# Attention, soft experts and a gated layer on one core: the gated layer's scale chain rewritten and its order of work redrawn

## The chip, the cores and the metric

One core of one Trainium2 chip runs the whole program. The metric is the time of one execution on the device in microseconds (us).

## What is computed

Three layers follow each other. Inputs of the first two are float32, the weights of the third are float64.

```python
# attention, 4 batches x 12 heads x 448 x 64, causal
scores = where(mask, -1e9, q @ k.T / 8);  attn = softmax(scores) @ v
x = attn as 1792 tokens x 768
# soft mixture: 8 experts x 4 slots
logits = x @ phi
slot_out[e] = relu((softmax(logits, 0).T @ x)[e] @ w1[e]) @ w2[e]     # 32 slots x 768
x = c @ slot_out,  c = softmax(logits, 1)                             # 1792 x 32
# gated layer, 1536 hidden columns
gate = sigmoid(x @ w_gate);  val = x @ w_val
out = (gate * val) @ w_out
```

## The kernel before, in words

The first 230 us are attention, the next 70 us the experts, whose weights stream in from memory, and the rest is the gated layer, which the change is about. The work of attention and of the gated layer is not written in the order in which it runs. A class `Plan` (L20) holds a list of operations, each with its engines and a cost in us, its dependencies, the buffers that it takes and a due time. `play` (L41) hands them out one by one and pins that order on each engine. For the gated layer a table `GSHIFT` (L163) shifts the due times, and with them the order; three numbers `SLACK, MARGIN, WAIT` set how due times go backwards and how far a later operation may be preferred. Costs and table decide the order and nothing else: on the chip each engine runs its list and waits where an operand or a buffer is late.

**The gated layer** runs over 6 units u of 256 hidden columns. Since x is c @ slot_out, the gate's and the value's weights are first multiplied with slot_out, once per unit:

- *Conversion.* Each unit has three weight blocks, o (w_out), v (w_val) and g (w_gate), of 1.5 MB float64. They land in a ring of five buffers (`ld`, by SP). ScalarE (`a1`, `a2`) and VectorE (`d1`, `d2`) turn each into float32 in place, four passes over 128x1536 words, which the trace shows as `w<-w`. A block's load waits until the block that had its buffer is used up: the load of unit 5's g block waits for `wlo` of unit 4.
- *Scale chain*, per unit: `psg` on TensorE (both products as four partial sums), `mv` on VectorE (largest absolute value of each row, for g and for v), `am2` (those two maxima as bf16), `one2` on TensorE (a matrix of ones times the maxima, so that each partition has the sum of all), `pw2` on VectorE (`pow2`, L251: the power of two below that sum, p, and the scale s = 2^14/p), then `ag` and `osc`, two small products of p for later. Beside it `gh` on ScalarE copies `psg` to SBUF and `fld` on TensorE folds the four partial sums. `sth` (ScalarE) and `stl` (VectorE) make of that sum a float16 pair, the tile `st`.
- For w_out: `absw` on ScalarE, `am` (its maximum as bf16), `one`, `pw`, then the float16 pair `whi` (ScalarE) and `wlo` (VectorE).
- *Hidden blocks.* Each unit has four batches b of 448 tokens with two blocks c of 128 hidden columns. `gv` on TensorE gives gate and value (`psg`, `psv` in the trace, 448 columns each), `sig` (ScalarE) the sigmoid, `hsv` (VectorE) the product `hs`, `hhi` (ScalarE) its upper half in float16 and `hlo` (GpSimd) the lower one. `hs` has two buffers, so a block's `hsv` waits for the `hlo` two blocks ahead of it.
- *Out-tiles.* 14 tiles i of 128 tokens: `outp` is 12 matmuls of 384 columns (`pso`), three products hhi·wh, hhi·wl and hlo·wh for both blocks. In unit 0 the first six come in two parts, with the hlo products last. Each half of the result is emptied by `evict`: in units 1 to 4 one half goes by ScalarE into a tile `ev` (two buffers), which `addp` on GpSimd adds to `oacc`, and the other half is added by VectorE. In the last unit both go by VectorE and each tile is stored.

Behind `psg` of unit 0, TensorE runs 20 products of ones (`psf`), which fill the wait for the first scale chain.

Of the kernel before, what the change touches and what calls it, by code (L numbers as in the profile page):

```python
# [101 lines left out]
def kernel(  # L102
# [60 lines left out]
    GSHIFT = {('a1', 1): 23.4, ('a1', 2): -6.21, ('a1', 3): 117.66, ('a1', 4): -5.02, ('a1', 5): 53.58, ('a2', 1):  # L163
              20.66, ('a2', 2): 118.34, ('a2', 3): 123.22, ('a2', 4): 79.78, ('a2', 5): 4.11, ('absw',): 36.12,
              ('addp', 1): 9.2, ('addp', 2): -5.3, ('addp', 3): -47.55, ('addp', 4): 58.74, ('am',): 1.36, ('am2',):
              -23.99, ('d1', 1): -180.16, ('d1', 2): 54.75, ('d1', 3): -2.65, ('d1', 4): -1.62, ('d1', 5): 30.01,
              ('d2', 1): 9.59, ('d2', 2): -33.11, ('d2', 3): -32.37, ('d2', 4): 8.67, ('d2', 5): 0.27, ('evict', 0):
              -148.33, ('evict', 1): -68.2, ('evict', 2): -111.03, ('evict', 3): -19.74, ('evict', 4): -31.48,
              ('evict', 5): 19.57, ('fl',): -9.57, ('fld',): 25.66, ('gh',): -29.78, ('gv', 0): -10.56, ('gv', 1):
              -235.77, ('gv', 2): -71.57, ('gv', 3): 21.32, ('gv', 4): 9.31, ('gv', 5): 8.04, ('hhi', 0): -461.87,  # L170
              ('hhi', 1): 83.0, ('hhi', 2): 5.44, ('hhi', 3): 25.33, ('hhi', 4): -7.65, ('hhi', 5): 9.17, ('hlo', 0):
              -0.95, ('hlo', 3): -9.74, ('hlo', 4): 42.9, ('hlo', 5): 20.64, ('hsv', 0): 17.3, ('hsv', 1): -5.98,
              ('hsv', 2): 0.18, ('hsv', 3): -20.78, ('hsv', 4): 18.54, ('hsv', 5): 4.2, ('ld', 1): -6.69, ('ld', 2):
              23.28, ('ld', 3): -32.29, ('ld', 4): -2.0, ('ld', 5): 39.32, ('mv',): -42.04, ('one',): -118.12,
              ('one2',): -17.53, ('outp', 0): 65.58, ('outp', 1): 1.02, ('outp', 10): 136.03, ('outp', 11): -0.62,
              ('outp', 12): -6.35, ('outp', 2): -3.63, ('outp', 3): 123.94, ('outp', 4): -8.45, ('outp', 5): -18.09,
              ('outp', 6): 218.04, ('outp', 7): -1.03, ('outp', 8): 231.97, ('outp', 9): 108.01, ('psg',): -384.17,
              ('pw',): -22.44, ('pw2',): -103.76, ('sig', 0): -240.48, ('sig', 1): -4.63, ('sig', 2): 27.87, ('sig',
              3): -144.49, ('sig', 4): -20.28, ('sig', 5): 17.06, ('sth', 0): -26.98, ('sth', 1): -11.12, ('sth', 2):
              -2.93, ('sth', 3): -40.58, ('sth', 4): -4.7, ('sth', 5): -0.58, ('stl', 0): 3.56, ('stl', 1): -0.2,  # L180
              ('stl', 2): 25.38, ('stl', 3): 8.1, ('stl', 4): -61.65, ('stl', 5): 13.43, ('store', 0): -10.25,
              ('store', 1): 15.69, ('store', 10): 2.55, ('store', 11): 55.39, ('store', 12): 11.05, ('store', 13):
              2.24, ('store', 2): 10.3, ('store', 3): 3.04, ('store', 4): -40.57, ('store', 5): 29.87, ('store', 6):
              7.57, ('store', 7): 43.43, ('store', 8): -4.75, ('store', 9): 49.48, ('whi',): -12.54, ('wlo',): 19.95}
# [1000 lines left out]
    def prep(u):  # L1185
        for nm in "ovg" if u else "":
# [22 lines left out]
        op((mv, u), call(mv), {"V": 0.8}, [(psg, u)], use=[p1])  # L1209
# [1 line left out]
        op((fld, u), call(fld), {"P": 0.9}, [(gh, u)], new=[("a", p2)], use=[h])
        op((am2, u), call(am2), {"V": 0.15}, [(mv, u)])
        op((one2, u), call(one2), {"P": 0.04}, [(am2, u)], new=[("b", x)])
# [90 lines left out]
```

## Time and profile before

| | |
|---|---|
| median of 3 runs | 519.91 us (519.75 to 521.16) |
| profiled execution, its own time | 519.79 us |
| its span in the profile | 518.0 us |
| TensorE busy, matmuls | 470.9 us (91%) |
| VectorE, ScalarE, GpSimd busy | 378.0, 341.4, 277.9 us |
| gated layer | about 300 to 518 us |

The span runs from the first to the last recorded instruction; the execution's own time has 1.8 us more around it. Nearly every gated instruction goes through one wrapper, line 244, so the rows are told apart by their tiles: `pso` is an out-tile, `w<-w` a conversion pass, `oacc` or `ev` an eviction, `mgv` is `mv`, `am` a cast of maxima, `gv4p` and `gv4s` the p and s of unit 4's pair, `o4p` and `o4s` those of its w_out. A row of the list in order of time gives start, duration, engine, operation, tiles out<-in, count, and in brackets the idle time before it with what ended it.

### The profile page before, as it was taken

What the parts mean: (1) busy time and instruction counts of PE and PEld (TensorE: products, weight loads), DVE (VectorE), ACT (ScalarE), POOL (GpSimd) and SP (SyncE); (2) the same over time, 40 slices, a digit from 0 to 9 for tenths busy, and PEclk for the clock granted to TensorE, in tenths of its full rate; (3) what the DMA queues carried; (4) which work ended last, traced back from release to release, by engine and by line L of the source; (5) the groups of instructions that cost most, each with busy time, mean ns of one, the idle gap of its engine ahead of it and who ended that gap; (6) DMA issues with size and microseconds to landing.
All of it is one profiled execution on the core that took longest, in us unless ns stands there. A gap on an engine that the chain in (4) does not pass through costs nothing.

```text
span 518.0 us, 12116 instructions
## 1 busy us (share of the span) xinstructions
PE 470.9 (91%) x4516; PEld 293.0 (57%) x4516; DVE 378.0 (73%) x920; ACT 341.4 (66%) x759; POOL 277.9 (54%) x371
## 2 busy tenths in 40 slices
PE   3899999999999999999837578999999998999997
PEld 2667767767667776655412234555455554555554
DVE  3889888989988987621055049899798998978564
ACT  3788887989887886111081059999897897686330
POOL 3088777787768812000000007249699997997530
PEclk9999999999999999999985999999999999999999
DMA  6866776762767357899999993360553320300145
GB/s 149 200 167 190 202 218 156 176 186 62 220 154 191 123 154 279 331 416 424 410 409 424 412 395 139 114 253 0 163 204 121 139 106 1 124 0 1 53 178 196
DMA packets 87531, 101.55 MB, mean 196 GB/s; under 512 B 68656, under 2 KB 68912, under 8 KB 85424
## 3 DMA queue, kind: packets, MB, share of 16 engines
q1 hardware_dynamic: 86544, 100.55, 57.4%
q8 instruction: 35, 0.57, 0.5%
q10 hardware_dynamic: 928, 0.23, 0.2%
q14 instruction: 24, 0.20, 0.1%
HBM read 95.26 MB, written 5.51 MB: 195 GB/s over the span
## 4 chain that ended last, share of the span: by engine, by line
PE 54%; POOL 15%; DMA 12%; DVE 6%; ACT 6%; issue 6%; SPq 1%; POOLq 0%; ACTq 0%; DVEq 0%
PE pso L244 11%; PE psP L244 8%; PE psS L244 8%; PE psV L244 7%; DMA w<-in_moe_w_gate_dram 5%; POOL hlo L244 5%; POOL oacc L244 5%; DMA w<-in_moe_w_dram 5%; POOL sq L244 4%; PE so L1069 3%; PE psT L244 3%; PE psh L1056 3%; PE psY L244 2%; PE psX L244 2%; ACT w L244 2%
## 5 line engine op out<-in xcount | busy, mean ns | idle before, releaser
L244 POOL TENSOR_TENSOR hlo<-hs,hhi 128x448 f16<-128x448 f32 x47 | 69.8, 1494 | 124.7 <-ACT hhi L244 124.6
L244 PEld LDWEIGHTS <-hhi 128*128 128x128 f16 x672 | 65.2, 98 | 51.1 <-issue 7.9
L244 ACT ACTIVATE P<-psS,nm 128x384 f32<-128x384 f32 (+3 forms) x168 | 82.1, 505 | 11.4 <-DVE nm L244 8.7
L244 PE MATMUL pso<-wh,hhi 128*128 128x384 f16 x336 | 82.7, 326 | 1.0 <-ACT oacc L244 0.5
L244 POOL TENSOR_TENSOR oacc<-oacc,ev 128x384 f32<-128x384 f32 x56 | 76.4, 1381 | 11.7 <-ACT ev L244 10.3
L244 PE MATMUL pso<-wh,hlo 128*128 128x384 f16 x336 | 81.6, 326 | 0.9 <-POOL hlo L244 0.9
L244 PE MATMUL pso<-wl,hhi 128*128 128x384 f16 x336 | 82.4, 326 | 0.0
L244 DVE CUSTOM_DVE_ANT_0 psS<-psS,cmaskq,sc 128x128 f32<-128x128 f32 (+2 forms) x144 | 62.8, 487 | 3.1 <-PE psS L244 2.4
L244 DVE SCALAR_TENSOR_TENSOR oacc<-pso,osc,oacc 128x384 f32<-128x384 f32 x84 | 50.1, 611 | 18.5 <-PE pso L244 18.2
L244 DVE SCALAR_TENSOR_TENSOR w<-w 128x1536 int32<-128x1536 int32 x30 | 62.0, 2067 | 0.7 <-ACT w L244 0.7
L244 PE MATMUL psP<-ident,P 128*128 128x128 f32 x384 | 59.4, 282 | 1.3 <-ACT P L244 1.3
L244 POOL TENSOR_TENSOR sq<-sq 112x512 bf16<-112x512 bf16 (+1 forms) x80 | 51.1, 639 | 6.0
L244 PEld LDWEIGHTS psP<-ident,P 128*128 128x128 f32 x384 | 42.9, 142 | 15.2 <-issue 8.8
L244 ACT COPY PT<-psP 128x512 f32<-128x512 f32 x83 | 46.7, 587 | 6.3 <-PE psV L244 5.2
L244 PE MATMUL psS<-qT,qT 64*64 64x256 f16 (+3 forms) x1008 | 48.9, 294 | 1.5 <-ACT qT L244 0.7
L244 ACT ACTIVATE w<-w 128x1536 int32<-128x1536 uint16 (+1 forms) x30 | 49.3, 1647 | 1.3 <-DMA w<-in_moe_w_gate_dram 1.3
L244 PE MATMUL psV<-PT,v 128*64 128x448 f32 (+3 forms) x384 | 46.8, 386 | 0.0
L244 ACT ACTIVATE ev<-pso,osc 128x384 f32<-128x384 f32 x56 | 32.7, 584 | 21.1 <-PE pso L244 11.1
L244 PEld LDWEIGHTS <-hlo 128*128 128x128 f16 x336 | 32.7, 98 | 23.2 <-POOL hlo L244 1.3
L327 DVE TENSOR_SCALAR hm<-psh,emask 128x256 f32<-128x256 f32 x8 | 5.3, 662 | 46.7 <-PE psh L1056 44.2
L244 PEld LDWEIGHTS <-qT 64*64 64x64 f16 x1008 | 28.2, 108 | 19.5 <-issue 7.0
L1064 ACT COPY hT<-psht 128x256 f32<-128x256 f32 x8 | 3.0, 372 | 53.6 <-PE psht L1062 46.8
(252 smaller groups left out, 847.7 us busy)
## 6 DMA issues: line engine op xcount, KB each, us to landing
w<-in_moe_w_dram SPq DMA_DIRECT2D x32, 1536.0 KB, 9.5
w<-in_moe_w_out_dram SPq DMA_DIRECT2D x6, 1536.0 KB, 11.8
w<-in_moe_w_val_dram SPq DMA_DIRECT2D x6, 1536.0 KB, 13.6
w<-in_moe_w_gate_dram SPq DMA_DIRECT2D x6, 1536.0 KB, 6.6
q<-in_q_dram SPq DMA_DIRECT2D x48, 112.0 KB, 3.3
k<-in_k_dram SPq DMA_DIRECT2D x46, 112.0 KB, 3.4
out_dram<-oacc SPq DMA_DIRECT2D x13, 384.0 KB, 2.3
v<-in_v_dram SPq DMA_DIRECT2D x36, 128.0 KB, 3.2
```

Of the source, the lines that this page charges most:

```text
L244: x = f(*a, **kw)
L327: nc.vector.tensor_scalar(to.rearrange("s (i q) -> s q i", i=2), ps.rearrange("s (q i) -> s q i", i=2), 0.0, emask[:, e:e + 1], ALU.max, A ...
L1056: nc.tensor.matmul(ps[32 * g:32 * g + 32, :], lhsT=slotT[:, kc, :], rhs=w[:, kc % 3, 256 * g:256 * g + 256], start=kc == 0, stop=kc == KC - 1)
L1064: nc.scalar.copy(hT, pt)
L1069: nc.tensor.matmul(so[32 * c:32 * c + 32, :], lhsT=hT[:, i, 32 * g:32 * g + 32], rhs=w[:, f % 4, 256 * c:256 * c + 256], start=e == 0 and ...
```

## The change

Six things are changed, all of them in the gated layer.

1. `pow2` works in PSUM: maximum, bit mask and reciprocal are written next to the ones' product, in the bank in which it landed, and only s goes to SBUF. The copy of p to SBUF is a fifth instruction, which for the pair g, v is put off into a new step `pw3`, with `ag` and `osc`.
2. `mv` writes its maxima as bf16, and `am2` is gone.
3. `am` (w_out's maximum as bf16) goes from VectorE to ScalarE.
4. `one2` is issued ahead of `fld`, always.
5. `sig` is planned behind `pw3`, since `ag` now comes from there.
6. The plan's costs, its three numbers and the table of shifts are new, so the whole order of the gated layer is drawn anew. The program up to `psg` of unit 0 keeps its order, but for unit 0's own w_out scale.

```diff
-    SLACK, MARGIN, WAIT = 1.252, 0.894, 0.49
-    GSHIFT = {('a1', 1): 23.4, ('a1', 2): -6.21, ('a1', 3): 117.66, ('a1', 4): -5.02, ('a1', 5): 53.58, ('a2', 1):
...
+    SLACK, MARGIN, WAIT = 0.213, 0.838, 0.347
+    GSHIFT = {('a1', 1): 46.98, ('a1', 2): 72.49, ('a1', 3): 117.45, ('a1', 4): 76.85, ('a1', 5): 11.54, ('a2', 1):
...
     def pow2(pool, mx, n, nm):
-
+        m, r = mx[:, :n], mx[:, n:]
         p = pool.tile([128, n], F32, tag=nm + "p", name=nm + "p")
         s = pool.tile([128, n], F32, tag=nm + "s", name=nm + "s")
-        on.ve.tensor_scalar(p, mx, 2.0 ** -20, None, ALU.max)
-        on.ve.tensor_scalar(p.bitcast(I32), p.bitcast(I32), 0x7F800000, None, ALU.bitwise_and)
-        on.ve.reciprocal(s, p)
-        on.ve.tensor_scalar(s, s, P14, None, ALU.mult)
-        return p, s
+        on.ve.tensor_scalar(m, m, 2.0 ** -20, None, ALU.max)
+        on.ve.tensor_scalar(m.bitcast(I32), m.bitcast(I32), 0x7F800000, None, ALU.bitwise_and)
+        on.ve.reciprocal(r, m)
+        on.ve.tensor_scalar(s, r, P14, None, ALU.mult)
+        return p, s, lambda: on.ve.tensor_copy(p, m)
...
     def am(nm, u):
         x = unit[u]["am", nm] = sm2.tile([128, 1], BF16, tag="am" + nm, name="am")
-        on.ve.tensor_copy(x, unit[u]["m", nm])
+        on.ac.copy(x, unit[u]["m", nm])
...
     def mv(u):
         d = unit[u]
-        d["mgv"] = sm2.tile([128, 2], F32, tag="mgv", name="mgv")
+        d["mgv"] = sm2.tile([128, 2], BF16, tag="mgv", name="mgv")
         on.ve.tensor_reduce(d["mgv"], d["ps"], axis=AX.X, op=ALU.max, apply_absolute_value=True)
-    def am2(u):
-        x = unit[u]["am2"] = sm2.tile([128, 2], BF16, tag="am2", name="am2")
-        on.ve.tensor_copy(x, unit[u]["mgv"])
-
     def one2(u):
-        x = unit[u]["x2"] = ps1.tile([128, 2], F32, tag="b", name="amx2")
-        on.te.matmul(x, lhsT=ones, rhs=unit[u]["am2"], start=True, stop=True)
+        x = unit[u]["x2"] = ps1.tile([128, 4], F32, tag="b", name="amx2")
+        on.te.matmul(x[:, :2], lhsT=ones, rhs=unit[u]["mgv"], start=True, stop=True)
     def pw2(u):
         d = unit[u]
-        p, r = pow2(sm2, d.pop("x2"), 2, f"gv{u}")
+        d["pgv"], r, d["f"] = pow2(sm2, d.pop("x2"), 2, f"gv{u}")
         for c, nm in enumerate("gv"):
-            d["p", nm], d["s", nm] = p[:, c:c + 1], r[:, c:c + 1]
+            d["s", nm] = r[:, c:c + 1]
+    def pw3(u):
+        d = unit[u]
+        d.pop("f")()
+        p = d["pgv"]
+        for c, nm in enumerate("gv"):
+            d["p", nm] = p[:, c:c + 1]
         d["ag"] = sm1(f"ag{u}")
         on.ve.tensor_scalar(d["ag"], p[:, 0:1], 2.0 ** -28, None, ALU.mult)
         osc(u)
...
-                op((am, u), lambda e: am("o", u), {"V": 0.15}, [(absw, u)])
+                op((am, u), lambda e: am("o", u), {"A": 0.2}, [(absw, u)])
...
+        op((one2, u), call(one2), {"P": 0.04}, [(mv, u)], new=[("b", x)])
+        op((fld, u), call(fld), {"P": 0.9}, [(gh, u)], new=[("a", p2)], use=[h], behind=[(one2, u)])
         op((pw2, u), call(pw2), {"V": 0.8}, [(one2, u)], use=[x])
+        op((pw3, u), call(pw3), {"V": 0.42}, [(pw2, u)], use=[x])
```

Three places show how rows move. The first is TensorE's list behind `psg` of unit 0, where `amx` is the ones' product `one2`, the `psg` made of `gh` is `fld`, and `psf` are the filling products.

```order
-L244 MATMUL psg_4744<-gh,fold_66 128x512
-L244 LDWEIGHTS ones
-L244 MATMUL amx_4751<-am_4749,ones 128x2
 L244 LDWEIGHTS ones
 L244 MATMUL psf<-ones 128x256
...
+L244 MATMUL amx_4751<-mgv,ones 128x2
+L244 MATMUL psg_4753<-gh,fold_66 128x512
```

The ones' product now takes `mgv` itself and stands ahead of the fold instead of behind it. Seven filling products stand ahead of the two and thirteen behind.

The second place is VectorE's list from the first hidden blocks of unit 0: `hs` is a hidden block, `w` a conversion pass, `hlo` a lower half. Before:

```order
L244 SCALAR_TENSOR_TENSOR hs<-psv,sg 128x448 x2
L244 SCALAR_TENSOR_TENSOR w<-w 128x1536
L244 TENSOR_TENSOR hlo<-hs,hhi 128x448
L244 SCALAR_TENSOR_TENSOR hs<-psv,sg 128x448 x2
L244 TENSOR_SCALAR oacc<-pso,osc_4763 128x384 x2
```

Now:

```order
L244 SCALAR_TENSOR_TENSOR hs<-psv,sg 128x448 x2
L244 SCALAR_TENSOR_TENSOR w<-w 128x1536
L244 SCALAR_TENSOR_TENSOR hs<-psv,sg 128x448
L244 SCALAR_TENSOR_TENSOR w<-w 128x1536
L244 SCALAR_TENSOR_TENSOR hs<-psv,sg 128x448
```

Batch 0's second `hlo` has left VectorE and runs on GpSimd behind the first one; a second conversion pass has come up into its place. On TensorE, `gv` of batch 2's first block now stands between the two parts of the first out-tile.

The third place is VectorE's list around the scale chain of unit 4, where the two `hs` are batch 3's blocks of unit 3. Before:

```order
L244 SCALAR_TENSOR_TENSOR hs<-psv,sg 128x448
L244 CAST am<-mo 128x1
L244 SCALAR_TENSOR_TENSOR oacc<-pso,osc_5920,oacc 128x384
L244 SCALAR_TENSOR_TENSOR hs<-psv,sg 128x448
L244 TENSOR_REDUCE mgv<-psg 128x2
L244 CAST am_6197<-mgv 128x2
L244 TENSOR_SCALAR o4p<-amx 128x1
```

Now:

```order
L244 SCALAR_TENSOR_TENSOR hs<-psv,sg 128x448
L244 SCALAR_TENSOR_TENSOR oacc<-pso,osc_5875,oacc 128x384
L244 TENSOR_REDUCE mgv<-psg 128x2
L244 SCALAR_TENSOR_TENSOR hs<-psv,sg 128x448
L244 TENSOR_SCALAR amx_6217<-amx_6217 128x2 x2
L244 RECIPROCAL amx_6217<-amx_6217 128x2
L244 TENSOR_SCALAR gv4s<-amx_6217 128x2
```

Both casts are gone from VectorE, `mv` stands ahead of the second block instead of behind it, and the pair's `pw2` comes before w_out's `pw`. In units 1 to 5 TensorE's list now has one shape: `psg`, one out-tile, `one2`, `fld`, `one` (in units 1 and 3 to 5 so, in unit 2 `one` ahead of `psg`), two out-tiles, and only then `gv` of the new unit. Before, it had one to three out-tiles there, in unit 4 w_out's `one` straight behind `psg`, and blocks of the old unit between.

## Rows read from the trace of the kernel before

**Rows 1.** Chain of waits that ended last: start us, us, what.

```profile
288.38 21.05 DMA w<-in_moe_w_gate_dram
...
402.35 0.19 PE psg L244
...
498.73 15.61 PE pso L244 x96
```

**Rows 2.** Busy time by stretch of the gated layer: PE, PEld, DVE, ACT, POOL, clock, DMA.

```profile
300.00:313.00 13.00, 9.37 (x67) 4.64 (x67) 7.11 (x17) 8.89 (x12) 2.42 (x1) 1.00 1.04 395
313.00:340.00 27.00, 26.45 (x170) 14.71 (x170) 25.00 (x42) 25.22 (x34) 10.31 (x6) 1.00 0.39 141
340.00:400.00 60.00, 57.06 (x365) 31.99 (x363) 53.11 (x74) 51.75 (x77) 50.20 (x34) 1.00 0.39 137
400.00:468.00 68.00, 65.15 (x416) 36.97 (x414) 59.77 (x88) 53.24 (x81) 62.67 (x45) 1.00 0.20 70
468.00:514.00 46.00, 46.00 (x280) 27.27 (x279) 30.29 (x52) 16.17 (x29) 19.32 (x18) 1.00 0.27 103
```

**Rows 3.** TensorE in order of time, 340 to 468 us: four of nine waits.

```profile
349.23 0.35 PE L244 MATMUL psv<-cT,st 128*128 128x448 f16 x1 [0.80 <-DVE hs L244]
...
366.32 0.16 PE L244 MATMUL amx<-am,ones 128*128 128x2 bf16 x1 [0.70 <-DVE am L244]
...
430.09 0.18 PE L244 MATMUL amx<-am,ones 128*128 128x1 bf16 x1 [0.99 <-DVE am L244]
...
466.98 0.16 PE L244 MATMUL amx<-am,ones 128*128 128x2 bf16 x1 [0.56 <-DVE o5p L244]
```

**Rows 4.** VectorE in order of time, around the scale chain of unit 4.

```profile
429.34 0.62 DVE L244 SCALAR_TENSOR_TENSOR hs<-psv,sg 128x448 f32<-128x448 f32 x1 [1.39 <-POOL hlo L244]
...
431.00 0.68 DVE L244 TENSOR_REDUCE mgv<-psg 128x2 f32<-128x512 f32 x1
431.71 0.53 DVE L244 CAST am<-mgv 128x2 bf16<-128x2 f32 x1
432.15 0.15 DVE L244 TENSOR_SCALAR o4p<-amx 128x1 f32<-128x1 f32 x1
...
434.10 0.75 DVE L244 TENSOR_SCALAR gv4s<-gv4s 128x2 f32<-128x2 f32 x1
```

**Rows 5.** Start of the gated layer in order of time: ScalarE, TensorE and VectorE.

```profile
303.80 1.59 ACT L244 ACTIVATE w<-w 128x1536 int32<-128x1536 uint16 x1
306.02 0.84 ACT L244 ACTIVATE st<-psg,gv0s 128x256 f16<-128x256 f32 x2 [0.62 <-DVE ag L244]
...
303.96 1.13 PE L244 MATMUL psg<-gh,fold 128*128 128x512 f32 x2 [0.93 <-ACT gh L244]
...
302.55 0.69 DVE L244 TENSOR_REDUCE mgv<-psg 128x2 f32<-128x512 f32 x1 [1.69 <-PE psg L995]
...
305.16 0.16 DVE L244 TENSOR_SCALAR gv0p<-amx 128x2 f32<-128x2 f32 x1 [1.71 <-PE amx L244]
...
305.75 0.17 DVE L244 TENSOR_SCALAR gv0s<-gv0s 128x2 f32<-128x2 f32 x1
...
309.94 1.75 DVE L244 SCALAR_TENSOR_TENSOR w<-w 128x1536 int32<-128x1536 int32 x1
...
312.64 0.98 PE L244 MATMUL pso<-wh,hlo 128*128 128x384 f16 x4 [0.92 <-POOL hlo L244]
```

**Rows 6.** GpSimd in order of time: lower halves.

```profile
310.17 2.42 POOL L244 TENSOR_TENSOR hlo<-hs,hhi 128x448 f16<-128x448 f32 x1 [89.21 <-ACT hhi L244]
...
330.80 1.03 POOL L244 TENSOR_TENSOR hlo<-hs,hhi 128x448 f16<-128x448 f32 x1 [6.30 <-ACT hhi L244]
```

**Rows 7.** Unit 5's last weight block: its issue, first pass and last pass.

```profile
445.39 0.37 SPq L244 DMA_DIRECT2D w<-in_moe_w_gate_dram  x1
...
451.99 1.64 ACT L244 ACTIVATE w<-w 128x1536 int32<-128x1536 uint16 x1 [1.27 <-DMA w<-in_moe_w_gate_dram]
...
460.09 2.07 DVE L244 SCALAR_TENSOR_TENSOR w<-w 128x1536 int32<-128x1536 int32 x1
```

More of the change, by code (lines that the diff above doesn't have):

```diff
@@ L161 @@
     LDT = 3.9
-    SLACK, MARGIN, WAIT = 1.252, 0.894, 0.49
-    GSHIFT = {('a1', 1): 23.4, ('a1', 2): -6.21, ('a1', 3): 117.66, ('a1', 4): -5.02, ('a1', 5): 53.58, ('a2', 1):
[L164 to L184, printed above, removed]
@@ new lines @@
+    SLACK, MARGIN, WAIT = 0.213, 0.838, 0.347
+    GSHIFT = {('a1', 1): 46.98, ('a1', 2): 72.49, ('a1', 3): 117.45, ('a1', 4): 76.85, ('a1', 5): 11.54, ('a2', 1):
[4 rows of a table added]
+              ('evict', 2): -10.86, ('evict', 3): -34.14, ('evict', 4): -69.36, ('evict', 5): 7.61, ('fl',): 56.11,
+              ('fld',): -18.46, ('gh',): -13.85, ('gv', 0): -4.49, ('gv', 1): 3.18, ('gv', 2): -181.43, ('gv', 3):
+              1.78, ('gv', 4): 13.45, ('gv', 5): 19.75, ('hhi', 0): -137.04, ('hhi', 1): -12.27, ('hhi', 2): 9.82,
+              ('hhi', 4): 30.01, ('hhi', 5): -19.56, ('hlo', 0): 12.02, ('hlo', 1): -12.39, ('hlo', 2): 11.6, ('hlo',
+              3): 42.46, ('hlo', 4): -4.81, ('hlo', 5): -10.46, ('hsv', 0): -215.65, ('hsv', 1): -20.97, ('hsv', 2):
+              -32.91, ('hsv', 3): 2.52, ('hsv', 4): -14.14, ('hsv', 5): -1.09, ('ld', 1): -54.47, ('ld', 2): -55.65,
+              ('ld', 3): -20.51, ('ld', 4): -20.82, ('ld', 5): 1.22, ('mv',): 8.18, ('one',): 78.0, ('one2',): -5.31,
+              ('outp', 0): 9.69, ('outp', 1): 231.96, ('outp', 10): 2.01, ('outp', 11): -19.17, ('outp', 12): 141.48,
+              ('outp', 13): 8.8, ('outp', 2): -15.32, ('outp', 3): -48.34, ('outp', 4): -62.9, ('outp', 5): 26.88,
+              ('outp', 6): 75.45, ('outp', 7): 145.39, ('outp', 8): 17.71, ('outp', 9): 48.86, ('psg',): -3.0,
+              ('pw',): 23.86, ('pw2',): -117.24, ('pw3',): 57.95, ('sig', 0): -5.71, ('sig', 1): -11.69, ('sig', 2):
+              63.57, ('sig', 3): 27.95, ('sig', 4): -4.24, ('sig', 5): 15.82, ('sth', 0): -36.3, ('sth', 1): -9.18,
+              ('sth', 2): 0.39, ('sth', 3): 52.37, ('sth', 4): -2.79, ('sth', 5): 34.01, ('stl', 0): -45.32, ('stl',
+              1): 23.57, ('stl', 2): -17.88, ('stl', 3): 6.66, ('stl', 4): -12.54, ('stl', 5): -38.8, ('store', 0):
+              -0.1, ('store', 1): 8.58, ('store', 10): 29.42, ('store', 11): 3.56, ('store', 12): 0.49, ('store', 13):
+              5.49, ('store', 2): 10.31, ('store', 3): -10.15, ('store', 4): 2.44, ('store', 5): 6.81, ('store', 6):
+              -18.28, ('store', 7): 15.16, ('store', 8): 12.44, ('store', 9): -24.06, ('whi',): 3.49, ('wlo',): 58.89}
@@ L972, in am @@
         x = unit[u]["am", nm] = sm2.tile([128, 1], BF16, tag="am" + nm, name="am")
-        on.ve.tensor_copy(x, unit[u]["m", nm])
+        on.ac.copy(x, unit[u]["m", nm])
     def one(nm, u):
-        x = unit[u]["x", nm] = ps1.tile([128, 1], F32, tag="b" if nm == "v" else "a", name="amx")
-        on.te.matmul(x, lhsT=ones, rhs=unit[u]["am", nm], start=True, stop=True)
+        x = unit[u]["x", nm] = ps1.tile([128, 2], F32, tag="b" if nm == "v" else "a", name="amx")
+        on.te.matmul(x[:, :1], lhsT=ones, rhs=unit[u]["am", nm], start=True, stop=True)
     def pw(nm, u):
         d = unit[u]
-        d["p", nm], d["s", nm] = pow2(sm2, d.pop(("x", nm)), 1, f"{nm}{u}")
+        d["p", nm], d["s", nm], f = pow2(sm2, d.pop(("x", nm)), 1, f"{nm}{u}")
+        f()
     def whi(u, e):
@@ L1208, in prep @@
            use=[("w", nm, u) for nm in "gv"] if u else [], due=1e9 if u else -100.0)
[L1209 removed]
+        op((mv, u), call(mv), {"V": 0.72}, [(psg, u)], use=[p1])
         op((gh, u), call(gh), {"A": 0.52}, [(psg, u)], new=[("gs", h)], use=[p1])
[L1211 to L1213 removed]
+        op((one2, u), call(one2), {"P": 0.04}, [(mv, u)], new=[("b", x)])
+        op((fld, u), call(fld), {"P": 0.9}, [(gh, u)], new=[("a", p2)], use=[h], behind=[(one2, u)])
         op((pw2, u), call(pw2), {"V": 0.8}, [(one2, u)], use=[x])
+        op((pw3, u), call(pw3), {"V": 0.42}, [(pw2, u)], use=[x])
         for nm in "gv":
@@ L1237 @@
                    behind=chained("gv", (gv,) + k))
-                op((sig,) + k, call(sig), {"A": 0.53}, [(gv,) + k], new=[("sg", ("sg",) + k)], use=[("pg",) + k])
+                op((sig,) + k, call(sig), {"A": 0.53}, [(gv,) + k, (pw3, u)], new=[("sg", ("sg",) + k)], use=[("pg",) + k])
                 op((hsv,) + k, call(hsv), {"V": 0.54}, [(sig,) + k], new=[("hs", ("hs",) + k)], use=[("pv",) + k, ("sg",) + k])
@@ L1241 @@
                    use=[("hs",) + k])
-                op((hlo,) + k, call(hlo), {"G": 1.35} if u or b else {"G": 1.35, "V": 0.62}, [(hhi,) + k], use=[("hs",) + k])
+                op((hlo,) + k, call(hlo), {"G": 1.45} if u or b else {"G": 1.3, "V": 0.62}, [(hhi,) + k], use=[("hs",) + k])
         if u == 0:
@@ L1265 @@
                 if a:
-                    op((addp, n) + k, call(addp), {"G": 1.3}, [(evict, n) + k], use=[("ev", n) + k], due=now + 2.5)
+                    op((addp, n) + k, call(addp), {"G": 1.36}, [(evict, n) + k], use=[("ev", n) + k], due=now + 2.5)
             if u == NU - 1:
```

4 lines of the change are left out of this document (2 added, 2 removed), and 4 rows, old and new, of the table GSHIFT.

## The prediction

> **What bounds the kernel now.** I read the chain of waits first. Up to about 300 us the change moves nothing that counts: attention keeps its order, and in the experts' stage the chain is a weight load of 21 us [rows 1]. From there on the chain is TensorE: one half of a `gv` takes 0.19 us, and at the end the 96 matmuls of eight out-tiles run through in 15.61, 1.95 a tile or 0.1625 a matmul [rows 1]. So the gated layer costs what TensorE has to do, plus what it waits. The table of busy time gives the size of that second part [rows 2]. In the last 46 us TensorE is busy all the time. From 340 to 400 it lacks 2.9 us (60 less 57.06), from 400 to 468 another 2.9 (68 less 65.15), from 313 to 340 only 0.6, and in the first 13 us 3.6. From 340 to 468 the idle time lies in nine waits, most of 0.6 to 1.0 us [rows 3]. A matmul counts as busy for 0.16 us longer than it keeps the next from starting (0.35 against 0.19 for `gv` [rows 1, 3]), so each wait costs 0.16 more than the row says: 5.8 plus 9 x 0.16 is **7.3 us**. That is the pot of the middle. The number of matmuls doesn't change, so nothing else is to be had there.
>
> What TensorE waits for says why. Three of the four rows shown are a ones' product that waits for a cast of maxima or for what stands around it; the fourth is a `gv` that waits for an `hs` to leave PSUM [rows 3]. Unit 4 shows the chain [rows 4]: VectorE stands 1.39 us for a lower half on GpSimd, then comes `mv` with 0.68, then the cast with 0.53, and later a multiplication of two columns with 0.75. The same kind of instruction on one column, `o4p`, takes 0.15, and at the start of the layer, where GpSimd is still idle, the two-column one takes 0.17 [rows 4, 5]. So two-column SBUF instructions are held up while GpSimd works, by 0.4 to 0.6 us each.
>
> [...]
>
> **The change part by part.**
>
> *Cast and PSUM.* The cast of the pair is gone and the other two-column steps read PSUM. The chain from `mv` to the scale loses 0.5 and 0.6 us where GpSimd works (0.53 less nothing, 0.75 less 0.17), and some 0.2, the cast, where it doesn't. What an instruction from PSUM to PSUM costs has no row. Its bounds: 0.15 (reading an SBUF column) and 0.69 (`mv`, which reads 512 columns of PSUM). The nearest is the first step of `pow2`, which reads PSUM already and takes 0.16 [rows 5], so I take 0.17 and a chain of 0.76, as now (305.16 to 305.92).
>
> [...]
>
> The copy of p, a fifth step, comes later in `pw3`, behind which only `sig` waits; `sig` comes after `gv`, so it lies beside other work. `am` on ScalarE is 0.2 us five times, in a queue that in the middle idles 8 us of 60 [rows 2]: nothing.
>
> *The start.* `mv` ends at 303.24, but the ones' product stands behind the fold, and `pow2` starts at 305.16 [rows 5]. Now the product follows `mv` at once, and s is there at about 304.4. `sth` can't use all of that: ScalarE's conversion pass ahead of it runs from 303.80 to 305.39 in both orders. So `sth` goes from 306.02 to 305.4: **0.6 us gained**, and with it the whole head of the layer.
>
> *The first lower halves.* Before, GpSimd made the first in 2.42 us beside VectorE's pass, and VectorE the second, so TensorE went on at 312.64 and was through with the first out-tile by 313.3 (4 x 0.1625). Now GpSimd makes both, the second under another pass. From the new start, 309.54, the first ends at 311.96. The second takes 1.03 free and 2.42 under a pass [rows 6]: 313.0 to 314.4. I take 2.42, since the list puts the pass right there. The last two matmuls then end at 314.7, and in the wait TensorE has done one `gv` block (0.38). Against 313.3 that is 1.0 us late net of the 0.6 gained: **+1.0**, with ends -0.3 and +1.1.
>
> *The chains of units 2 to 4.* Now each has one out-tile between `psg` and `one2`, and two between `fld` and `gv`. For unit 4, by durations of rows: ahead of `mv` VectorE has an `hs` and an eviction (0.6 each), which are through by the end of `psg` or up to 0.8 later if a lower half ran under a pass. With `mv` that is 0.7 to 1.5 us after `psg`, and TensorE asks for it after 1.95. So the wait in front of `one2` goes, with 0.4 to spare. From `one2` to `gv` TensorE has the fold (1.13 in the row, of which the last 0.16 overlaps: 1.0 [rows 5]) and two tiles, 4.9 us. ScalarE needs a pass (1.6 [rows 5]), an eviction and an `hhi` (about an `hs` each, 0.6 [rows 4]) and then `sth` (0.84), some 3.7 us; the two `stl` with an eviction between them, again as an `hs` each and half overlapping, take 1.5 more, 5.2. That leaves **0.3 us** of waiting in each of the three units.
>
> *Unit 5.* Its g block is loaded when `wlo` of unit 4 is through, which the new order has behind tile 11's eviction instead of tile 9's. Now, from the issue at 445.39 to the end of the last pass at 462.16 go 16.8 us [rows 7], and TensorE just doesn't wait. With eight tiles and six `gv` blocks between instead of nine and five, the cover is 1.6 us shorter (17.9 for 19.5); with fewer instructions between the passes, the need is about 1.2 shorter, which leaves 0.4 to wait. ScalarE, which stood 1.27 for the load, now has an out-tile's eviction right behind the pass; I put another 0.4 for the tiles that this holds, **0.8** in all. `mv` of unit 5 still stands behind both `hs`, each behind a lower half: another **0.75**.
>
> *What moves besides.* Loads and stores keep their order on SP, the last unit's tiles follow one another, and the last 46 us have no wait to lose [rows 2].
>
> **The sum.** From the profiled execution, 519.8: +1.0 for the start, -7.3 for the pot, +2.5 for the waits that I find in the new order (3 x 0.3, 0.8, 0.75) gives 516.0. The median of the runs is 0.1 higher than that execution, so **516.1**. Small gaps below 0.3 us, which I didn't follow, are left as they are.
>
> **The rivals.**
>
> *No change.* The waits only move. In the middle VectorE is busy 88%, GpSimd 84 to 92% [rows 2]; a chain that comes earlier only meets the next late thing, such as a `gv` half whose bank an `hs` has not yet left (the 0.80 at 349.23 [rows 3]). For it: the busy shares. Against: three of the four waits shown stand at the chains themselves. If half of the pot's 4.8 us of net gain returns in mid-unit and the start costs 1.1, the time is 518.6; if three quarters return, 519.8.
>
> *Slower: GpSimd holds VectorE, and VectorE holds `mv`.* Place: the chains of units 2 to 5, where `hs` waits for one of two buffers, and GpSimd must first finish one or two additions and the lower half. Each of them that runs under a conversion pass takes 1.4 us more (2.42 less 1.03). My slack in front of `one2` is 0.4: one such meeting beyond those that I counted costs 1.0 a chain and takes back the gain (4 x 1.0, 520.1), two cost 2.4. From about 1.5 a chain on, the change is slower; with two in two chains and one in the others it is 516.1 + 6.8 = 522.9. For it: the wait of 1.39 [rows 4], and GpSimd has one more lower half. Against: the chains' passes now end before `psg`.
>
> *Better.* No new wait in units 2 to 5, and the second lower half gets through before the pass: 519.9 - 7.3 - 0.3 = 512.3. That takes a half that starts first and a pass that waits for it; no row shows it for this pair.
>
> *It doesn't do what it says*: PSUM steps are held up by GpSimd as well, or cost 0.69 each. Then `s` comes 2 us later, `gv` by 1.7 a unit, 5 x 1.7 = 8.5: 524.6. I put little on it, by the row of 0.16.
>
> **How the numbers follow.** A measurement of this kernel can tell 0.3%, 1.6 us. Forecast 516.1 with 514 to 518.3: 0.58. Better, 512.3: 0.12. No change: 0.16, a fifth of it below 518.3. Slower by GpSimd: 0.11; by PSUM: 0.03. Faster by over 0.3% is then 0.58 + 0.12 + 0.02, some 0.72; same 0.14, slower 0.14. The range from 513.0 to 520.8 leaves out half of the better case and the slower ones.
>
> **What would show it.** In the new profile: `amx` within 0.2 us of `mv`'s end where TensorE is free; `gv0s` and its like at 0.15 to 0.2 everywhere; `sth` of unit 0 at about 305.4; a wait of TensorE of some 2 us for GpSimd at 312; no wait over 0.5 in front of `amx` in units 2 to 4. From 340 to 468 the idle time should fall from 5.8 to about 2. Wrong would be the forecast if TensorE's idle time there stays above 4, whichever the releaser, or if a `gv` waits for `stl` over 0.5 in every unit.

## The result and the profile after

The changed kernel takes 515.09 us (median of 9 runs, 513.93 to 518.82) against 519.91 before (9 runs, 518.82 to 521.21), a ratio of 0.9916, 95% interval 0.9891 to 0.9941. Forecast were 516.1 us, 513.0 to 520.8, and faster by over 0.3% with 0.72. It is faster by 0.6 to 1.1%. One of the ten executions of variant e8 below took 617.81 us, at a mean granted clock of 0.75 instead of 0.97 to 0.99, and is left out of its median.

The profiled execution of the new kernel took 516.78 us, its span 515.0. That is 3.0 us under the span before, but the gated layer gained more: `psg` of unit 0 starts at 302.49 us instead of 300.92, because the experts' weights landed later in this execution (TensorE's last product of the experts, which waits for them in both, starts at 299.19 us instead of 297.62). Over all profiles of this study the same point lies between 299.5 and 303.8, though the programs are the same up to there. So from here on times are counted **from the start of `psg` of unit 0**. There the last out-tile ends at 213.42 us before and at 208.85 now: **4.57 us gained**. Each unit's share can be read from the first `gv` of the unit, corrected by 1.95 us for each out-tile that TensorE has done more or fewer by then:

| first `gv` of unit | 0 | 1 | 2 | 3 | 4 | 5 | end |
|---|---|---|---|---|---|---|---|
| before, us | 6.51 | 36.94 | 68.31 | 101.27 | 136.36 | 175.12 | 213.42 |
| now, us | 5.77 | 33.81 | 70.63 | 100.15 | 134.06 | 168.61 | 208.85 |
| out-tiles ahead, before / now | 0 / 0 | 11 / 9 | 23 / 25 | 36 / 37 | 50 / 51 | 66 / 65 | |
| lead of the new kernel | 0.74 | -0.77 | 1.58 | 3.07 | 4.25 | 4.56 | 4.57 |

The start loses, units 2 to 4 win, unit 5 adds little. The table of busy time says the same (columns as in [rows 2]; from 313 to 340 us TensorE now lacks 2.1 us, where it lacked 0.6):

```profile
300.00:313.00 13.00, 10.40 (x84) 5.17 (x76) 6.21 (x15) 7.95 (x12) 2.00 (x1) 1.00 1.04 394
313.00:340.00 27.00, 24.92 (x158) 13.65 (x158) 24.45 (x39) 24.69 (x37) 12.93 (x9) 1.00 0.40 147
340.00:400.00 60.00, 59.79 (x387) 34.27 (x386) 52.01 (x74) 53.61 (x81) 50.44 (x36) 1.00 0.35 121
400.00:465.00 65.00, 63.03 (x407) 36.09 (x405) 57.50 (x80) 53.64 (x83) 59.65 (x42) 1.00 0.23 84
465.00:511.00 46.00, 46.00 (x280) 27.23 (x278) 30.37 (x60) 16.77 (x29) 20.64 (x20) 1.00 0.27 103
```

TensorE now lacks 0.2 us from 340 to 400, where it lacked 2.9, and 2.0 instead of 2.9 up to 465: 2.2 in place of 5.8. From 312 us on, three of its waits over 0.5 us are left, here in order of time on TensorE:

```profile
314.13 0.35 PE L244 MATMUL psv<-cT,st 128*128 128x448 f16 x1 [1.38 <-DVE hs L244]
...
431.66 0.16 PE L244 MATMUL amx<-mgv,ones 128*128 128x2 bf16 x1 [0.39 <-DVE mgv L244]
...
456.05 0.48 PE L244 MATMUL pso<-wh,hhi 128*128 128x384 f16 x2 [1.46 <-ACT ev L244]
```

With the 0.16 that a matmul's record overlaps they cost 1.54, 0.56 and 1.62 us. The chain of unit 4, shown before in [rows 4], is now this on VectorE:

```profile
430.91 0.69 DVE L244 TENSOR_REDUCE mgv<-psg 128x2 bf16<-128x512 f32 x1 [1.39 <-ACT gh L244]
431.52 0.61 DVE L244 SCALAR_TENSOR_TENSOR hs<-psv,sg 128x448 f32<-128x448 f32 x1
432.05 0.36 DVE L244 TENSOR_SCALAR amx<-amx 128x2 f32<-128x2 f32 x2
432.45 0.18 DVE L244 RECIPROCAL amx<-amx 128x2 f32<-128x2 f32 x1
432.66 0.16 DVE L244 TENSOR_SCALAR gv4s<-amx 128x2 f32<-128x2 f32 x1
```

From `mv`'s start to the end of s it takes 1.91 us, with an `hs` in between; it took 3.85 (431.00 to 434.85), with w_out's own steps in between. And none of the steps in PSUM was held up anywhere, as the groups of `amx` on VectorE show (count: shortest/median/longest in ns, first and last start):

```profile
L244 DVE TENSOR_SCALAR amx<-amx x22: 151/168/169, 305.1 to 469.6; 128x2 f32<-128x2 f32 x6, 128x2 int32<-128x2 int32 x6, 128x1 f32<-128x1 f32 x5, 128x1 int32<-128x1 int32 x5
L244 DVE RECIPROCAL amx<-amx x11: 176/178/179, 305.5 to 469.8; 128x2 f32<-128x2 f32 x6, 128x1 f32<-128x1 f32 x5
```

### The profile page after: what moved, and what is told of

The parts are those of the page before. It is cut to its first block, busy times and chain, and to the rows that moved or that the text cites. A ratio compares the mean times of both kernels' runs of the same rounds, so it can differ in the third digit from the quotient of the medians.

```text
span 515.0 us, 12119 instructions
## 1 busy us (share of the span) xinstructions
PE 467.0 (91%) x4516; PEld 292.3 (57%) x4516; DVE 373.1 (72%) x917; ACT 343.1 (67%) x767; POOL 278.7 (54%) x372
## 4 chain that ended last, share of the span: by engine, by line
PE 54%; POOL 15%; DMA 14%; DVE 6%; ACT 5%; issue 4%; SPq 0%; POOLq 0%; ACTq 0%; DVEq 0%
PE pso L244 18%; PE psP L244 7%; PE psS L244 6%; PE psV L244 6%; DMA w<-in_moe_w_dram 6%; POOL sq L244 6%; DMA w<-in_moe_w_val_dram 5%; POOL hlo L244 5%; POOL oacc L244 4%; PE psT L244 3%; DMA q<-in_q_dram 3%; PE so L1073 2%; PE psg L244 2%; PE psY L244 2%; PE psX L244 2%
## 5 line engine op out<-in xcount | busy, mean ns | idle before, releaser
L244 POOL TENSOR_TENSOR hlo<-hs,hhi 128x448 f16<-128x448 f32 x48 | 71.7, 1505 | 119.4 <-ACT hhi L244 119.0
L244 DVE SCALAR_TENSOR_TENSOR w<-w 128x1536 int32<-128x1536 int32 x30 | 63.7, 2122 | 1.5 <-ACT w L244 1.4
```

Of the source, the lines that this page charges most:

```text
L244: x = f(*a, **kw)
```

## The experiments

All variants run an explicit list, one `engine:operation` after the other, in place of the planner's choice; without further edits it is the new kernel, instruction for instruction. "End" is the end of the last out-tile after `psg` of unit 0, from one profile each. The ratio is to executions of the kernel before that ran alongside each variant, with medians from 518.93 to 519.91 us.

| kernel | end, us | median, us (runs) | ratio to before, interval |
|---|---|---|---|
| before | 213.42 | 519.91 (9) | |
| new kernel | 208.85 | 515.09 (9) | 0.9916 [0.9891, 0.9941] |
| e1 old steps, new order | 212.43 | 518.15 (12) | 0.9985 [0.9965, 1.0005] |
| e2 new steps, old order | 212.91 | 518.77 (12) | 0.9992 [0.9976, 1.0007] |
| e3 fold ahead of the ones' product | 210.38 | 516.10 (5) | 0.9929 [0.9907, 0.9951] |
| e4 lower half back on VectorE | 208.72 | 515.54 (4) | 0.9926 [0.9903, 0.9950] |
| e5 load of unit 5's g earlier | 208.52 | 514.26 (6) | 0.9900 [0.9879, 0.9921] |
| e6 e4 and e5 together | 208.01 | 514.69 (6) | 0.9913 [0.9882, 0.9943] |
| e7 e1 with one-column steps | 209.84 | 516.27 (8) | 0.9934 [0.9900, 0.9969] |
| e8 cast back | 209.74 | 516.13 (9) | 0.9943 [0.9921, 0.9965] |
| e9 steps back in SBUF | 211.36 | 518.88 (10) | 0.9995 [0.9978, 1.0012] |
| e10 `am` back on VectorE | 209.87 | 514.45 (6) | 0.9920 [0.9892, 0.9948] |
| e11 e6 and `mv` ahead of `gh` | 207.47 | 513.46 (6) | 0.9894 [0.9871, 0.9917] |
| e12 the new kernel again | 208.83 | 514.88 (6) | 0.9927 [0.9902, 0.9951] |

By their intervals only e1, e2 and e9 are slower than the new kernel; those of all other variants overlap its own. So what the other ends say rests on one trace each, not on the time. The ends of the new kernel's two traces (e12 is the second) agree within 0.02 us.

One thing has to be known to read the ends. Ahead of `psg` of unit 1, two conversion passes on VectorE meet two lower halves on GpSimd. In e1, e3, e5 and e10 that meeting fell the other way than in the new kernel; unit 1's first `gv` then comes 0.55 us later, for a reason that is not their edit (last section). In e5 the order up to there is the new kernel's; for the other three I infer it from the same pattern. For these four I also give the end less 0.55.

### Order or steps: e1 and e2

e1 is the kernel before, all its steps, in the new kernel's order; e2 the new kernel with the order of before.

```diff
 # e1: from before
-    pl.play()
+    pl.seq = """ P:psg.0 P:fl.0 P:fl.1 V:mv.0 V:am2.0 A:gh.0 P:fl.2
...
+ V:mv.1 V:am2.1 G:hlo.3.0.0 A:gh.1 V:am.1 A:a1.v.2 P:one2.1 G:hlo.3.0.1 P:fld.1 V:pw2.1
...
+    """.split()
+    pl.play()
 # e2: from after
-    pl.play()
+    pl.seq = """ P:psg.0 P:fl.0 P:fl.1 V:mv.0 A:gh.0 P:fl.2 P:fl.3 P:fld.0
...
```

> Order of the changed kernel, instruction by instruction, but the old steps: maxima in float32 with the cast behind them, powers of two in SBUF, w_out's cast on VectorE, p made at once. Measured from the start of psg of unit 0 to the end of the last matmul's eviction, before takes 213.4 us and the change 208.9. Theory A (the steps count because two-column SBUF instructions are held by GpSimd, and the new order leaves little spare time): in units 2 to 5 some 0.5 us come back in front of each ones' product and 0.3 to 0.6 in front of gv; 211 to 212, some 2 to 3 us slower than the change, about 517.5. Rival B (the order alone gives the gain, its spare time covers the casts): 208.9 to 209.4, 515 to 515.6.

> New steps (maxima as bf16, powers of two in PSUM, w_out's cast on ScalarE, p copied right behind) in the order of the kernel before. Theory A (steps count): the waits in front of ones' products in units 4 and 5 lose 0.5 to 1 us each, the start 0.2; 211 to 212 us from psg of unit 0 to the end against 213.4 and 208.9, about 518. Rival B (the order alone): 213 to 213.4, 519.5 to 520.

e1 ends at 212.43 (211.9 less the meeting), e2 at 212.91: the order alone gains 1.0 (1.5) us, the steps alone 0.5, both together 4.57. In time neither can be told from before. e1 lies at the upper end of its theory A or above it, e2 between its two expectations. e1 shows where the order without the steps loses: TensorE waits 1.22 for unit 4's `amx` and 2.32 in unit 5. In e2 the steps are as fast as in the new kernel, but the waits have other causes there (1.15 for an `hs` at 350.68, 0.94 in front of unit 3's `amx`, again behind an `hs`). One wait in e2 comes from a new step itself: `am` now stands on ScalarE behind a conversion pass of 1.58 us, and w_out's `one` of unit 1 waits for it, 1.11 with the overlap, where before nothing waited:

```profile
334.66 0.16 PE L253 MATMUL amx<-am,ones 128*128 128x1 bf16 x1 [0.95 <-ACT am L253]
```

Without it the steps alone could have gained up to 1.6 (an estimate, 0.5 and 1.11; it was not run). That and the order's 1.5 still leave 1.5 of the 4.57. So **a good part of the gain is neither part's own: the order lays the chains where their length decides, and the steps make them short.**

### Which step: e8, e9, e10 and e7

```diff
 # e8: from after; am2 stands behind mv in VectorE's list
-        d["mgv"] = sm2.tile([128, 2], BF16, tag="mgv", name="mgv")
+        d["mgv"] = sm2.tile([128, 2], F32, tag="mgv", name="mgv")
...
+        on.ve.tensor_copy(x, unit[u]["mgv"])
...
-        on.te.matmul(x[:, :2], lhsT=ones, rhs=unit[u]["mgv"], start=True, stop=True)
+        on.te.matmul(x[:, :2], lhsT=ones, rhs=unit[u]["am2"], start=True, stop=True)
 # e9: from after
-        on.ve.tensor_scalar(m, m, 2.0 ** -20, None, ALU.max)
-        on.ve.tensor_scalar(m.bitcast(I32), m.bitcast(I32), 0x7F800000, None, ALU.bitwise_and)
-        on.ve.reciprocal(r, m)
-        on.ve.tensor_scalar(s, r, P14, None, ALU.mult)
+        on.ve.tensor_scalar(p, m, 2.0 ** -20, None, ALU.max)
+        on.ve.tensor_scalar(p.bitcast(I32), p.bitcast(I32), 0x7F800000, None, ALU.bitwise_and)
+        on.ve.reciprocal(s, p)
+        on.ve.tensor_scalar(s, s, P14, None, ALU.mult)
 # e10: from after
-        on.ac.copy(x, unit[u]["m", nm])
+        on.ve.tensor_copy(x, unit[u]["m", nm])
 # e7: from e1; likewise for the three other steps and the cast
-        on.ve.tensor_scalar(p, mx, 2.0 ** -20, None, ALU.max)
+        for k in range(n):
+            q, t, m = p[:, k:k + 1], s[:, k:k + 1], mx[:, k:k + 1]
+            on.ve.tensor_scalar(q, m, 2.0 ** -20, None, ALU.max)
```

> The new kernel with one step undone: mv writes float32 again and the cast of the pair stands behind it, held 0.5 to 0.65 us in units 3 to 5. Theory (the chain of each unit counts only where TensorE has no slack in front of amx): unit 4, which already waits 0.56 there, loses all of its 0.6, units 2, 3 and 5 have up to 0.5 of slack, so end at 209.4 to 210.2 us after psg of unit 0 (now 208.85). Rival, losses of the three steps add up to the 3.6 us that e1 has over the new kernel, a third or more for this one: 210.2 to 210.8. Third: no loss at all, 208.9.

> The new kernel with pow2 back in SBUF (maximum, mask, reciprocal and scale as before, no copy of p), the cast still gone and am still on ScalarE. Theory: s comes 0.6 us later in units 2 to 5, and the two out-tiles and the fold ahead of gv hide most of it: end at 209.0 to 210.0 us after psg of unit 0 (now 208.85). Rival (losses add up): 210 to 210.8.

> The new kernel with the one-column am of w_out back on VectorE, at the same place in the list of the program. Theory: its row takes 0.15, but it stands in VectorE's queue and holds what is behind it, or comes late itself; e1 showed one wait of 1.22 us in front of unit 4's one-column amx, so end at 209.5 to 210.5 us after psg of unit 0 (now 208.85). Rival: 0.15 us more on VectorE costs nothing, 208.8 to 209.0, and e1's wait there came from the held pair.

> Old steps in the new order, as in e1, but the cast of the pair and the pair's four steps are made one column at a time in SBUF (10 instructions on 128x1 instead of 5 on 128x2). Theory: what is held beside GpSimd is the two-column form; one-column instructions never are. Then each takes 0.14 to 0.17 us, no am and no gv4s row over 0.2, and the end comes at 209 to 210.5 us after psg of unit 0, where e1 has 212.43 and the new kernel 208.85, although there are twice as many instructions. Rival: whatever reads and writes SBUF at that place is held, by its place in the order; then rows of 0.5 and more remain and the end is at 212.4 or later.

Undoing one step costs 0.89 us (e8), 2.51 (e9) and 1.02 (e10, 0.5 less the meeting). The steps in PSUM are the largest part, and the only one of the three that the time shows too: e9 can't be told from the kernel before, although its end comes 2.06 us earlier than there, and e10's median (514.45) is no longer than the new kernel's. In e9 the mask and the scale of unit 4's pair are held again; the reciprocal between them, also of two columns in SBUF, is not:

```profile
434.21 0.15 DVE L253 TENSOR_SCALAR gv4p<-amx 128x2 f32<-128x2 f32 x1
434.40 1.03 DVE L253 TENSOR_SCALAR gv4p<-gv4p 128x2 int32<-128x2 int32 x1
435.46 0.17 DVE L253 RECIPROCAL gv4s<-gv4p 128x2 f32<-128x2 f32 x1
435.66 0.72 DVE L253 TENSOR_SCALAR gv4s<-gv4s 128x2 f32<-128x2 f32 x1
```

I had put the loss of e9 at 1.2 us at most, since two out-tiles and the fold cover the chain in front of `gv`. That cover held (0.87 lost up to unit 4's `gv`). The rest came behind it, by two ways. TensorE met two evictions that were not through, 0.43 at 439.36 and 0.64 at 442.68 us, where the new kernel has no such waits. And `wlo` of unit 4 stands behind these steps on VectorE, so the load of unit 5's g block was issued 2.6 us later (at 450.07 with `psg` of unit 0 at 303.81, against 446.17 and 302.49), and TensorE's wait for unit 5 grew from 1.62 to 2.16.

e8 fits the first theory: unit 4, which had no slack, waits 1.24 instead of 0.56 for `amx`, unit 5 0.42 for its own, and the other chains only give up slack. The expectation of e10 misread e1: the product that waited there is the pair's, of two columns, behind the held cast,

```profile
430.72 0.16 PE L253 MATMUL amx<-am,ones 128*128 128x2 bf16 x1 [1.05 <-DVE am L253]
```

and in e10 unit 4 waits 0.56, as in the new kernel. What `am` on VectorE may cost shows in unit 5 (2.10 for 1.62), in this one trace.

e7 names the property that matters. The casts in e1, and in e7, which does the same work in SBUF with twice as many instructions:

```profile
L253 DVE CAST am<-mgv x6: 171/481/636, 301.8 to 466.3; 128x2 bf16<-128x2 f32 x6
L253 DVE CAST am<-mo x5: 138/139/145, 328.6 to 462.4; 128x1 bf16<-128x1 f32 x5
```

```profile
L253 DVE CAST am<-mgv x12: 145/152/157, 301.9 to 464.1; 128x1 bf16<-128x1 f32 x12
```

One at a time, no step is held, in the same places beside the same work on GpSimd, and the end comes 2.6 us earlier than in e1 (2.0 less the meeting). Of e7's 36 casts and scalar steps of the pairs from SBUF to SBUF, 25 ran wholly while GpSimd was busy and took 145 to 157 ns. In e1 every such two-column step took 0.24 to 0.79 us beside GpSimd and 0.17 where GpSimd was idle; in the kernel before they took 0.20 to 0.93 and 0.17. So in these traces it is the two-column form from SBUF to SBUF that is held (casts and scalar operations, one of them 1.03 us in e9; not the reciprocal, 0.17), not SBUF or the place. By what means GpSimd holds it, no run shows. That the same steps escape in PSUM (0.17) and at one column (0.15) is what e9 against the new kernel, and e7, show.

### The start: e3 and e4

```diff
 # e3: TensorE's list, from after
-P:fl.5 P:fl.6 P:one2.0 P:fld.0
+P:fl.5 P:fl.6 P:fld.0 P:one2.0
 # e4: the first lower halves and gv of batch 2, from after
-G:hlo.0.0.1
+V:hlo.0.0.1 V:hsv.1.0.0
-P:outp.a.0.0 P:gv.2.0.0 P:outp.0.0
+P:outp.a.0.0 P:outp.0.0 P:gv.2.0.0
```

> The changed kernel with one swap: in unit 0 the fold is issued ahead of the ones' product again. If the 0.6 to 0.7 us of the start come from this swap, sth of unit 0 goes back from 4.4 to about 5.0 us behind psg (the cast that is gone keeps 0.2) and the first gv from 5.8 to 6.4; the rest shifts with it, 209.5 from psg to the end. Rival: the cast alone gave it, then nothing moves by over 0.1.

> The changed kernel with the second lower half of batch 0 back on VectorE, behind the first conversion pass, and gv of batch 2's first block back behind the first out-tile. If that move is what cost the start about 1.0 us net of the gain of 0.7, the gv that follows psg of unit 1 comes at 33.0 us behind psg of unit 0 instead of 33.8, and the end at 208.1. Rival: the start is held by the hs buffers and by the conversion passes on VectorE that psg of unit 1 needs; then TensorE's 1.4 us wait at the first gv goes, but psg of unit 1 stays at 25.1 or moves later, and the end stays at 208.9 or is later.

With the fold first the first `gv` comes at 6.60 instead of 5.77, 0.83 late where 0.6 was expected, and the end is 1.0 later less the meeting: what the start gains is kept to the end. In e4 the old handling of the lower halves comes back, TensorE again waits 0.92 for GpSimd as in [rows 5], and nothing changes: `psg` of unit 1 starts at 25.15 instead of 25.13, the end is 208.72. **The move of the lower half, which I had priced, costs nothing.** What sets that stretch stands on VectorE in both, the passes ahead of `psg` of unit 1 (in the new kernel the last two end at 327.52, and `psg` starts at 327.62).

### The waits that were left: e5, e6, e11

```diff
 # e5: VectorE's list, from after: wlo of unit 4 and d2 of unit 5's v block change places
-V:d2.v.5
+V:wlo.4
...
-V:wlo.4
+V:d2.v.5
 # e11: from e6 (e5 and e4 together)
-A:gh.4 P:outp.3.6 V:mv.4
+P:outp.3.6 V:mv.4 A:gh.4
-P:psg.5 A:evict.0.4.5 V:evict.1.4.5 G:addp.0.4.4 A:hhi.3.4.0 V:hsv.3.4.1 A:gh.5 P:outp.4.6 V:mv.5
+P:psg.5 V:mv.5 A:evict.0.4.5 V:evict.1.4.5 G:addp.0.4.4 A:hhi.3.4.0 A:gh.5 V:hsv.3.4.1 P:outp.4.6
```

> The new kernel with one swap in VectorE's order: wlo of unit 4 ahead of the second VectorE pass of unit 5's v block, so that the load of unit 5's g block, which waits for wlo, is issued some 3 us earlier. Theory: the wait of ScalarE for this load (2.42 us) and TensorE's wait of 1.62 us behind it at 456 both vanish: end at 207.2 to 207.5 us after psg of unit 0 (now 208.85), time 513.5. Rival: the pass of the v block, which now ends 2 us later, becomes the new wait, in front of psg of unit 5: end at 208.5 or later, no gain.

> The swap of the load and the old start together (second lower half of batch 0 on VectorE, gv of batch 2 behind the first out-tile). Theory: the swap's gain of 1.5 us and the start's 0.1 add up, end at 207.0 to 207.4 us after psg of unit 0, time 513.3. Rival: the start's shift of VectorE's order puts some later chain late, end at 208 or later.

> Both earlier edits (the load swap and the old start), and in units 4 and 5 the maxima mv ahead of the copy gh in the order in which the program hands them out; in unit 5 mv also ahead of the last eviction and the second hs. Theory: mv and gh read the same PSUM tile, and the one handed out second waits for the other to end, so TensorE's two waits in front of amx (0.57 in unit 4, 0.58 in unit 5) come from that order and vanish: end at 206.8 to 207.3 us after psg of unit 0, where the kernel with both earlier edits has 208.01, and a time of 512.9 to 513.5. Rival: mv then waits for the late hs and its lower half instead, one or both waits stay, and the end is at 207.5 or later.

In the new kernel ScalarE stood for unit 5's g block, with the eviction that TensorE needed right behind the pass:

```profile
453.91 1.62 ACT L244 ACTIVATE w<-w 128x1536 int32<-128x1536 uint16 x1 [2.42 <-DMA w<-in_moe_w_gate_dram]
455.42 0.57 ACT L244 ACTIVATE ev<-pso,osc 128x384 f32<-128x384 f32 x1
```

In e5 the load goes out 2.9 us earlier and both waits are gone, ScalarE's 2.42 and TensorE's 1.62. But 0.58 appears in front of unit 5's `amx`, where there was none, so the end is 208.0 less the meeting, 0.9 earlier where 1.4 and more were expected. The rival's cause is not it: `psg` of unit 5 came 0.9 earlier, not later. e6 gains 0.7 over e4 in the same way; its 208.01 is what its rival named, but not for the start's sake.

That wait and the 0.56 of unit 4 led to e11. `mv` and `gh` read the same `psg`, and in every unit of the new kernel the one handed out second starts only behind the end of the first, by 0.03 us in units 1 and 3 to 5 (0.08 in unit 0, 0.18 in unit 2). In unit 4 VectorE was free at 429.5, but `gh` ran on ScalarE from 430.29 to 430.88, and `mv` started at 430.91. Why one reader waits for the other, no run shows. With `mv` first, both waits vanish on TensorE in e11:

```profile
427.79 0.49 PE L253 MATMUL pso<-wh,hlo 128*128 128x384 f16 x2
428.12 0.17 PE L253 MATMUL amx<-mgv,ones 128*128 128x2 bf16 x1
...
461.49 0.49 PE L253 MATMUL pso<-wh,hlo 128*128 128x384 f16 x2
461.81 0.17 PE L253 MATMUL amx<-mgv,ones 128*128 128x2 bf16 x1
```

The swap of the two readers is the cause in unit 4 only. In unit 5 `mv` had waited just 0.06 us for `gh`; it stood behind an `hs` that waited for a lower half and, behind that, the second `hs`, and e11 moves it ahead of these too. In e6:

```profile
463.08 0.62 DVE L253 SCALAR_TENSOR_TENSOR hs<-psv,sg 128x448 f32<-128x448 f32 x1 [1.38 <-POOL hlo L253]
...
464.83 0.69 DVE L253 TENSOR_REDUCE mgv<-psg 128x2 bf16<-128x512 f32 x1
```

The end comes 0.54 earlier than in e6, not the 1.15 that the two waits cost, and lies between the two expectations. Unit 4's `gv` came 0.56 earlier, but `psg` of unit 5 did not: TensorE met two evictions that were not through, one by VectorE (0.46) and one by ScalarE (0.30). So unit 4's gain was given back to the next bound, and what the end keeps is unit 5's. e11 has the shortest trace, 5.95 us under before; its interval in time overlaps that of the new kernel.

### The new kernel again: e12

```diff
-    pl.play()
+    pl.seq = """ P:psg.0 P:fl.0 P:fl.1 V:mv.0 A:gh.0
...
```

> The new kernel once more, instruction for instruction, for its spread. Four of the nine variants with the new order show psg of unit 1 0.85 us later (26.0 instead of 25.13 us after psg of unit 0), with VectorE's last two passes ahead of it at 5.1 instead of 4.25 us. Theory: that is no effect of their edits but a meeting of passes and lower halves that falls one way or the other from run to run; then this one lies at 25.1 or at 26.0, with its end at 208.8 or about 209.4. Rival: the edits cause it; then 25.13 and 208.85 exactly as before.

It repeats the first profile within 0.1 us at each landmark (25.16 and 208.83 for 25.13 and 208.85), so it did not show the other outcome and settles nothing by itself. What speaks for a meeting is e5, whose list is that of the new kernel up to unit 4 and which yet had 26.01 at unit 1.

## Why the prediction was right, and where not

*The pot.* Right: TensorE's idle time from 340 on fell from 5.8 to 2.2 us, where "about 2" was forecast. The sum too: I had 3.8 us of gain in all, the gated layer gained 4.57, the medians differ by 4.8.

*Cast and PSUM.* Right in price and in kind: 0.17 a step, no hold-up. A pair's four steps take 0.76 to 0.78 us in every unit (I had 0.76); before, they took 1.34 to 1.54 in units 1 and 3 to 5. In the new order SBUF would have cost more than the 0.6 that I priced: in e9 they take 1.42 to 2.17 in units 2 to 5, since the mask is held as well. That a two-column step in PSUM runs on beside a busy GpSimd was my assumption, with no row for it in the prediction; in the new kernel such steps of units 2 to 5 took 0.16 to 0.18 us each with GpSimd at work beside them. The rival of held or dear PSUM steps fell with the row of 22 at 151 to 169 ns. Two rows were misread, without harm to the sum. The `o4p` of [rows 4], my one-column instruction and lower bound, reads PSUM (`o4p<-amx`), so it could not tell one column from PSUM; e7 does. And the load of 21 us in [rows 1] is the gated layer's `w_gate`, not an experts' weight.

*The start.* The gain of `sth` was 0.72 for 0.6 (306.87 is 4.38 after `psg` of unit 0, 306.02 was 5.10). The net was -0.77 where I had -1.0, but **the cause that I gave is wrong**: "I take 2.42, since the list puts the pass right there". The two lower halves on GpSimd took 3.42 together, the second ran free (1.04) and the pass took longer (2.05, where the one beside the first half took 1.75), as the case that I called better wanted it:

```profile
311.00 3.42 POOL L244 TENSOR_TENSOR hlo<-hs,hhi 128x448 f16<-128x448 f32 x2 [90.71 <-ACT hhi L244]
```

```profile
313.45 0.62 DVE L244 SCALAR_TENSOR_TENSOR hs<-psv,sg 128x448 f32<-128x448 f32 x1 [0.93 <-POOL hlo L244]
314.00 2.05 DVE L244 SCALAR_TENSOR_TENSOR w<-w 128x1536 int32<-128x1536 int32 x1
```

TensorE waited all the same, 1.38 instead of 0.92, because `gv` of batch 2 needed a bank that this `hs` had not yet emptied, and the `hs` waited for the first half's buffer. The wait of some 2 us for GpSimd, which I had named as a sign, did not come. But e4 undoes the move and stays as late. What holds unit 1 is VectorE's passes, which I left out of this stretch: where they end 0.9 us later, `psg` of unit 1 starts 0.9 later. So it is luck that -0.77 lies near my -1.0.

*Units 2 to 4.* I had 0.3 for each `gv` and 0.4 to spare in front of `one2`. No `gv` waited for `stl`; the spare was there in units 2 and 3, and in unit 4 it was -0.56. The step that failed is "ahead of `mv` VectorE has an `hs` and an eviction": it left out that `mv` also stands behind `gh` when `gh` comes first in the list.

*Unit 5.* I had 0.8 for the load and 0.75 in front of `amx`, 1.55 together; measured was 1.62, in one place, so the sum is near by luck. The load's wait was twice what I said, and it made the other vanish, since the chain ran on meanwhile. e5 shows the second one behind it: without the first, 0.58.

*The rivals.* "No change" describes e1 and e2, each half of the change alone. The slower rival's waits exist (an `hs` stood 0.94 us for a lower half at 394.76, in unit 3's chain, and 1.38 at 463.68, in unit 5's), but over 1 us in unit 5 only, and TensorE waited for neither. For the better case, 512.3, waits would have had to vanish that are still there; e11 takes two of the three large ones out and comes to 513.5.

## What to carry to other kernels

Shortening a chain pays only where the order lets somebody wait for it, and an order pays only if the chains it relies on are short: each alone gave 0.5 to 1.5 us here, both 4.6. A cast or scalar operation on 128x2 from SBUF to SBUF beside a busy GpSimd took 0.20 to 0.93 us in the kernel before, instead of 0.17; a scalar operation in PSUM took 0.15 to 0.17 in the new kernel, and one column at a time in SBUF 0.15 to 0.16 in e7. A wait that stands at the head of a chain hid the next one in e5 (1.62 us went, 0.58 came): before pricing its removal, work out what is late behind it.
